# Attention with a gated MLP on one core: turned blocks of p loaded two steps later, the opening reordered, z1 products begun with the last scores, and a scratch of the inverse square root in PSUM

## The chip, the cores and the metric

The kernel runs on one core of one Trainium2 chip. A core has a matrix engine (TensorE, PE in the rows; its weight loads are PEld), VectorE (DVE), ScalarE (ACT), GpSimd (POOL) and SyncE (SP). They run side by side and meet through semaphores; each carries out its own instructions in program order. In this kernel all bulk transfers are issued by SP, which writes a DMA into a queue and goes on, unless the DMA first has to wait for something. The metric is the time on the device in microseconds (us), as the median of several runs; the profile is one execution of its own.

## What is computed

The input x has 2048 rows of 512 floats. Its layer norm goes into two branches, an attention of 32 heads over the last 512 cached keys (W is 512), and a gated MLP that mixes over the rows with a 2048 x 2048 matrix. The result joins them.

```python
def _A_ref(x, k_cache, v_cache, wq, wo):
    q = (x @ wq).reshape(B, Sq, Hq, Dh).transpose(0, 2, 1, 3)
    k, v = k_cache[:, :, Sk - W:], v_cache[:, :, Sk - W:]
    scores = jnp.einsum("bhqd,bhkd->bhqk", q, k) * (Dh ** -0.5)
    p = _softmax(scores, axis=-1)
    o = jnp.einsum("bhqk,bhkd->bhqd", p, v)
    return o.transpose(0, 2, 1, 3).reshape(B, Sq, Hq * Dh) @ wo

def _B_ref(x, w_in, w_sp, b_sp, w_out):
    z = _gelu(jnp.einsum("bsd,df->bsf", x, w_in))
    z1 = z[..., :Fh]
    z2 = _layernorm(z[..., Fh:], axis=-1)
    g = jnp.einsum("ts,bsf->btf", w_sp, z2) + b_sp[None, :, None]
    return jnp.einsum("bsf,fd->bsd", z1 * g, w_out)

xn = _layernorm(x, axis=-1)
s = _A_ref(xn, A_k_cache, A_v_cache, A_wq, A_wo)
g = _silu(_B_ref(xn, B_w_in, B_w_sp, B_b_sp, B_w_out))
return x + s * g
```

## The kernel before

**Products.** All operands are float32. Each is split into a high part (rounded to fp32r by a copy on ACT) and a low part (what is left, a subtraction on POOL or DVE, line 56), and each product is made of three on PE: high by high, high by low, low by high (`mm3`, lines 60 to 62). That is why every product below comes in threes, and why every operand needs one ACT and one POOL or DVE instruction first.

**Layout of the program.** Its five parts follow one another in code order.

1. The opening (lines 296 to 348): x is loaded into `sacc`, 16 tiles of 128 rows. `ln_stats` takes mean and variance on DVE, `rsqrt` lays out a chain of small DVE instructions (two to four elements a partition) for the inverse root, and `tick` lets a few of them go between larger work. `ln_apply` normalizes in place, `ln_flip` transposes on PE and splits into xh (ACT) and xl (DVE). `z1_piece(i, 0)` makes the first of two column halves of tile i's z1; `gelu` is applied to it much later. `split_piece` makes high and low parts of a piece of a weight that `load_piece` had brought into a buffer `raw`.
2. The step loop (lines 350 to 385), t from -7 to 532. A head has 4 blocks of 512 rows, a block 4 steps; there are 512 steps that have a score. A full step holds twelve products of 512 columns: three of `qproj` for the block 7 steps ahead, three of `score`, three of `pv` (12 steps behind) and three of `outp` (17 behind). Pieces of the weights have their own table (lines 289 to 294): piece k of head h is split at step 16 h plus an offset, and its load is issued eight steps earlier.
3. The z stage (lines 444 to 457): 16 tiles, two halves of 344 columns each. `z_product` on PE, `z_gelu` on ACT with the statistics on DVE, and for each pair of tiles `z_norm`: the chain of the inverse root, then two `tensor_scalar` (line 437). `z_split` makes z_h on ACT and z_l on POOL.
4. The mix stage: the 2048 x 2048 matrix by z2 in `mix`, into new PSUM pools that take the place of the old ones, so the first products wait until the z stage's PSUM tiles have been read.
5. The end of each row tile: gate, transposes, `project`, silu, out.

**The way of p.** A score's softmax numerator `prob` (ACT) has to be transposed before it can be a weight of `pv`. `turn(t - 1)` (lines 228 to 243), the last thing in step t, transposes 32 x 32 squares on DVE into a buffer `pB` (four of them) and issues its write to a DRAM block `p_dram`. After the fourth tile of a block it also issues four loads (line 242) that gather the whole block into `pL` (two buffers, 1 MB each). `shares` (ten steps behind a score) splits one quarter of pL into pT_h (ACT) and pT_l (POOL), and `pv` uses it two steps later. The four loads wait for the block's last write to land. SP carries out its instructions in order, so all that stands behind them waits as well: the next writes, the loads of weight pieces, the writes of s and z1.

**The output sum.** `outp` goes into a PSUM tile, and DVE adds it into `sacc`, scaled by the row's softmax sum (line 276). A PSUM tile of `ps_step` (four of them) is free when that has been done, and scores, outp and the z1 products share them.

**z1's second half.** From step `Z1` on, one `z1_piece(t - Z1, 1)` stands in each step (line 373): twelve products of 344 columns, a copy on ACT, a write to DRAM that SP issues (line 197). Before, `Z1` is NSTEP + 2, 514. `turn` still comes after it in the same step, as `pv` and `outp` run on to the end of the loop.

## Time and profile before

| | |
|---|---|
| median of 3 runs | 1937.86 us (1936.36 to 1940.21) |
| the profiled execution | 1932.73 us, its span 1931.0 |
| DVE busy | 1314.0 us, 68%, 2336 instructions |
| ACT busy | 1023.2 us, 53%, 2199 instructions |
| POOL busy | 944.3 us, 49%, 742 instructions |
| SP's DMA queue | 355.33 MB, 70.6% of 16 engines' span |
| granted clock of PE, mean | 0.997 |

The span runs from the first to the last instruction. The matrix engine's share stands with the prediction. Products are pipelined, so a row's duration on PE is longer than the distance from one product to the next; the pace is read from start times. In the timeline a row gives start, duration, engine, line, operation, what it writes and reads, the tile's form, how many equal ones were joined (x4), and in brackets how long the engine had been idle just before and what released it. In the list of waits a row gives the engine and line that waited, what it waited for, the total in us, how many times, and the longest. `SPq` and `PEld` are SP's issue of DMAs and PE's weight loads. The windows give, for a stretch of time, each engine's busy time, then PE's clock, the share in which the DMA engines were busy, and GB/s. The names of tiles in rows are those of the program: `ps` stands for tiles of `ps_step` and, by name, `ps_a` for those of `ps_acc`.

### The profile page before, as it was taken

What the parts mean: (1) busy time and instruction counts of PE and PEld (TensorE: products, weight loads), DVE (VectorE), ACT (ScalarE), POOL (GpSimd) and SP (SyncE); (2) the same over time, 40 slices, a digit from 0 to 9 for tenths busy, and PEclk for the clock granted to TensorE, in tenths of its full rate; (3) what the DMA queues carried; (4) which work ended last, traced back from release to release, by engine and by line L of the source; (5) the groups of instructions that cost most, each with busy time, mean ns of one, the idle gap of its engine ahead of it and who ended that gap; (6) DMA issues with size and microseconds to landing.
All of it is one profiled execution on the core that took longest, in us unless ns stands there. A gap on an engine that the chain in (4) does not pass through costs nothing.

```text
span 1931.0 us, 28085 instructions
## 1 busy us (share of the span) xinstructions
PE 1889.9 (98%) x8914; PEld 1580.9 (82%) x8914; DVE 1314.0 (68%) x2336; ACT 1023.2 (53%) x2199; POOL 944.3 (49%) x742
## 2 busy tenths in 40 slices
PE   6999999999999999999999999999999999999999
PEld 6778878788887788787887777777877898999998
DVE  7678877878877787877787787787887383111112
ACT  3456656556655556656565565555665343324332
POOL 1155555555555555555555555555555155322320
PEclk9999999999999999999999999999999999999999
DMA  4588888888888888888888888878888504333321
GB/s 162 148 213 221 204 214 218 211 209 211 214 212 215 210 214 222 205 210 219 213 207 217 209 207 211 220 201 210 224 206 209 188 28 146 119 102 106 122 70 51
DMA packets 393509, 357.12 MB, mean 185 GB/s; under 512 B 21856, under 2 KB 290400, under 8 KB 393360
## 3 DMA queue, kind: packets, MB, share of 16 engines
q1 hardware_dynamic: 393360, 355.33, 70.6%
q8 instruction: 69, 1.13, 0.3%
q14 instruction: 80, 0.66, 0.1%
HBM read 207.00 MB, written 148.24 MB: 184 GB/s over the span
## 4 chain that ended last, share of the span: by engine, by line
PE 72%; DMA 11%; DVE 8%; ACT 3%; issue 3%; SPq 1%; POOL 0%; DVEq 0%; ACTq 0%; POOLq 0%
DMA p_dram<-pB 10%; PE ps L60 10%; PE ps L61 9%; PE ps L62 9%; PE ps_a L60 9%; PE ps_a L61 9%; PE ps_a L62 9%; PE ps_g L60 4%; PE ps_g L62 4%; PE ps_g L61 4%; DVE pB L234 2%; DVE nm L224 2%; ACT prob L226 2%; DVE sacc L276 2%; PE ps_f L60 1%
## 5 line engine op out<-in xcount | busy, mean ns | idle before, releaser
L56 POOL TENSOR_TENSOR pT_l<-pL,pT_h 128x512 fp32r<-128x512 f32 x507 | 655.4, 1293 | 617.3 <-ACT pT_h L249 553.4
L226 ACT ACTIVATE prob<-ps,nm 128x512 f32<-128x512 f32 x512 | 353.0, 689 | 560.3 <-DVE nm L224 560.3
L234 DVE STREAM_TRANSPOSE pB<-prob 128x512 f32<-128x512 f32 x512 | 359.9, 703 | 102.9 <-DMA p_dram<-pB 102.2
L276 DVE SCALAR_TENSOR_TENSOR sacc<-ps,sums,sacc 128x512 f32<-128x512 f32 x496 | 364.5, 735 | 23.4 <-PE ps L62 22.1
L224 DVE TENSOR_REDUCE nm<-ps 128x1 f32<-128x512 f32 x512 | 334.8, 654 | 1.0 <-PE ps L62 0.8
L249 ACT CAST pT_h<-pL 128x512 fp32r<-128x512 f32 x512 | 316.1, 618 | 21.5 <-DMA pL<-p_dram 15.4
L56 POOL TENSOR_TENSOR wl<-raw,wh 128x512 fp32r<-128x512 f32 (+1 forms) x144 | 180.6, 1256 | 88.3 <-ACT wh L138 88.3
L60 PE MATMUL ps<-wh,qT_h 128*128 128x512 f32 x512 | 211.6, 413 | 10.8 <-DVE sacc L276 8.0
L61 PE MATMUL ps_a<-pT_l,wh 128*128 128x512 f32 x512 | 200.5, 392 | 4.1 <-POOL pT_l L56 4.1
L61 PE MATMUL ps<-wl,qT_h 128*128 128x512 f32 x512 | 201.7, 394 | 0.0
L60 PE MATMUL ps<-wh,oT_h 128*128 128x512 f32 x512 | 199.9, 390 | 1.3 <-ACT z L196 1.1
L60 PE MATMUL ps_a<-xh,wh 128*128 128x512 f32 x512 | 200.4, 391 | 0.0
L60 PE MATMUL ps_a<-pT_h,wh 128*128 128x512 f32 x512 | 199.9, 390 | 0.5 <-ACT pT_h L249 0.5
L61 PE MATMUL ps_a<-xl,wh 128*128 128x512 f32 x512 | 200.1, 391 | 0.0
L62 PE MATMUL ps<-wh,qT_l 128*128 128x512 f32 x512 | 199.7, 390 | 0.0
L62 PE MATMUL ps_a<-xh,wl 128*128 128x512 f32 x512 | 199.6, 390 | 0.0
L61 PE MATMUL ps<-wl,oT_h 128*128 128x512 f32 x512 | 199.6, 390 | 0.0
L62 PE MATMUL ps_a<-pT_h,wl 128*128 128x512 f32 x512 | 199.2, 389 | 0.0
L62 PE MATMUL ps<-wh,oT_l 128*128 128x512 f32 x512 | 198.9, 389 | 0.0
L60 PE MATMUL ps_g<-z_h,xh 128*128 128x344 f32 x512 | 167.4, 327 | 4.4 <-ACT z L425 4.4
L62 PE MATMUL ps_g<-z_h,xl 128*128 128x344 f32 x512 | 164.2, 321 | 0.0
L61 PE MATMUL ps_g<-z_l,xh 128*128 128x344 f32 x512 | 164.0, 320 | 0.0
(107 smaller groups left out, 3059.2 us busy)
## 6 DMA issues: line engine op xcount, KB each, us to landing
p_dram<-pB SPq DMA_DIRECT2D x512, 256.0 KB, 6.1
pL<-p_dram SPq DMA_DIRECT2D x512, 256.0 KB, 5.2
raw<-wh SPq DMA_DIRECT2D x128, 256.0 KB, 6.4
raw<-w_sp SPq DMA_DIRECT2D x56, 256.0 KB, 3.3
z_dram<-z SPq DMA_DIRECT2D x32, 172.0 KB, 1.9
z<-z_dram SPq DMA_DIRECT2D x16, 344.0 KB, 3.2
s_dram<-sacc SPq DMA_DIRECT2D x16, 256.0 KB, 2.0
s_t<-s_dram SPq DMA_DIRECT2D x16, 256.0 KB, 3.5
```

Of the source, the lines that this page charges most:

```text
L56: engine.tensor_tensor(lo, whole, hi.bitcast(F32), op=OP.subtract)
L60: nc.tensor.matmul(ps, lh, rh, start=first, stop=False)
L61: nc.tensor.matmul(ps, lh, rl, start=False, stop=False)
L62: nc.tensor.matmul(ps, ll, rh, start=False, stop=last)
L224: nc.vector.tensor_reduce(nm, ps, axis=AX.X, op=OP.max, negate=True)
L226: nc.scalar.activation(prob[t], ps, AF.Exp, bias=nm, accum_out=sums[b][:, j:j + 1])
L234: nc.vector.transpose(pB.rearrange("p (k q) -> p k q", q=Q), prob.pop(t))
L249: nc.scalar.copy(h, p)
L276: nc.vector.scalar_tensor_tensor(sacc[:, i, :], ps, rs, sacc[:, i, :], op0=OP.mult, op1=OP.add)
```

## The change

It has five parts.

- **Loads of turned blocks.** The four loads of pL leave `turn` and become `turned(b)`. It is called where t is 2 modulo 4, ahead of that step's own `turn`. `turn` of a block's fourth tile stands in the step in which t is 0 modulo 4, so two steps lie between. `shares` and `pv` keep their steps.
- **The inverse root.** `rsqrt` gets its scratch from outside, in two halves, `here` and `there`, and each instruction reads one operand of each. It has thirteen instructions, for one element as for more (eight for one before, eleven for two or more). In the opening both halves are SBUF. In the z stage `there` is a PSUM tile, `tmps`, taken from `ps_acc`. So the z products no longer use `ps_acc`: all of them go through the four tiles of `ps_step`.
- **The opening.** Groups of x tiles are 1, 1, 2, 4, 4, 4 instead of 1, 1 and pairs. The first pieces of w_in and of head 0 have their low parts made on DVE instead of POOL, and the statistics run further ahead (i + 6 for i + 4). The pieces 1 to 3 of head 0 are split inside the step loop, at steps -5, 6 and 9.
- **z1 and the pieces of w_in.** `Z1` is NSTEP - 3, 509, and the write of a z1 piece is issued by ACT. The pieces of w_in for z1's second half and for the z stage are loaded and split at other steps, and share the buffers of other numbers (`FOLLOWS`).
- **Constants.** `halves` and `magic` become one tile `consts`, and a copy of them stands in `tmps`.

```diff
@@ -78,32 +78,32 @@
-    def rsqrt(pool, var, n):
-        v = pool.tile([P, 4], F32, name="rs_v", bufs=6)
-        y = pool.tile([P, 4], F32, name="rs_y", bufs=6)
-        a = pool.tile([P, 4], F32, name="rs_a", bufs=6)
-        v, y, a = v[:, :n], y[:, :n], a[:, :n]
+    def rsqrt(var, y, n, here, there, consts_here, consts_there):
+        (y0, y1, a0), (v, u, a1) = ([m[:, k * n:k * n + n] for k in range(3)] for m in (here, there))
+        stt, mul = nc.vector.scalar_tensor_tensor, nc.vector.tensor_mul
         chain = []
         chains.append(chain)
         def add(f, *args, **kw):
             chain.append(lambda: f(*args, **kw))
-        stt = nc.vector.scalar_tensor_tensor
-        add(stt, v, var, EPS, halves[:, :n], op0=OP.add, op1=OP.mult)
-        add(stt, y.bitcast(I32), v.bitcast(I32), -0.5, magic[:, :n], op0=OP.mult, op1=OP.add)
-        for _ in range(3):
-            if n == 1:
-                add(stt, a, y, v, y, op0=OP.mult, op1=OP.mult)
-            else:
-                add(nc.vector.tensor_mul, a, y, y)
-                add(nc.vector.tensor_mul, a, a, v)
-            add(stt, y, a, 1.5, y, op0=OP.subtract, op1=OP.mult)
-        return y, chain
+        add(stt, v, var, EPS, consts_there[:, :n], op0=OP.add, op1=OP.mult)
+        add(stt, y0.bitcast(I32), v.bitcast(I32), -0.5, consts_here[:, 4:4 + n], op0=OP.mult, op1=OP.add)
+        add(mul, u, v, y0)
+        for old, new in ((y0, y1), (y1, y0), (y0, y)):
+            add(mul, a1, u, old)
+            add(stt, new, a1, 1.5, old, op0=OP.subtract, op1=OP.mult)
+            if new is not y:
+                add(mul, a0, u, old)
+                add(stt, u, a0, 1.5, u, op0=OP.subtract, op1=OP.mult)
+        return chain
+    def set_consts(t):
+        nc.vector.memset(t[:, :4], 0.5)
+        nc.vector.memset(t[:, 4:], float(0x5F3759DF - (1 << 22) - (1 << 31)))
@@ -130,17 +130,21 @@
+    FOLLOWS = {("w", 1): (0, 1, 0, 2), ("w", 2): (1, 3, 2, 3), ("w", 3): (0, 1, 0, 2)}
     def split_piece(key, k, engine):
         n = 512 if key[0] == "h" else NB
-        hi = wp.tile([P, 512], F32R, name=f"wh{k}")
-        lo = wp.tile([P, 512], F32R, name=f"wl{k}")
+        f = FOLLOWS[key][k] if key in FOLLOWS else k
+        hi = wp.tile([P, 512], F32R, name=f"wh{f}")
+        lo = wp.tile([P, 512], F32R, name=f"wl{f}")
         r = raw.pop((key, k))[:, :n]
         nc.scalar.copy(hi[:, :n], r)
         rest(engine, lo[:, :n], r, hi[:, :n])
         wt[key, k] = (hi, lo)
-    GROUPS = [(0, 1), (1, 2)] + [(a, a + 2) for a in range(2, NT, 2)]
+    GROUPS = [(0, 1), (1, 2), (2, 4)] + [(a, a + 4) for a in range(4, NT, 4)]
@@ -149,14 +153,16 @@
     def ln_stats(i):
         a, b = next(g for g in GROUPS if g[0] <= i < g[1])
...
         if i == b - 1:
-            r, chain = rsqrt(stats, mv[a][:, :b - a, 1], b - a)
+            r = stats.tile([P, 4], F32, name="rs_r", bufs=4)
+            here, there = (stats.tile([P, 12], F32, name=f"rs_{k}", bufs=3) for k in range(2))
+            chain = rsqrt(mv[a][:, :b - a, 1], r[:, :b - a], b - a, here, there, consts, consts)
             for j in range(a, b):
                 rx[j] = mv[a][:, j - a, 0:1], r[:, j - a:j - a + 1], chain
@@ -194,7 +200,7 @@
         zmm(ps[:, :NB], i, n, range(2, NC))
         z = zs.tile([P, NB], F32, name="z1")
         nc.scalar.copy(z, ps[:, :NB])
-        nc.sync.dma_start(z1_dram[:, i, n * NB:(n + 1) * NB], z)
+        nc.scalar.dma_start(z1_dram[:, i, n * NB:(n + 1) * NB], z)
@@ -236,11 +242,13 @@
             pD[b] = dram.tile([4, P, 512], F32, name="p_dram", bufs=3)
         nc.sync.dma_start(pD[b][j], pB)
         if j == 3:
-            pL[b] = ap.tile([P, 16, P], F32, name="pL")
-            of = pD.pop(b).rearrange("j (i r) (a f) -> a r (j i) f", i=4, a=4)
-            for a in range(4):
-                nc.sync.dma_start(pL[b][Q * a:Q * a + Q], of[a])
             nc.vector.reciprocal(sums[b], sums[b])
+    def turned(b):
+        pL[b] = ap.tile([P, 16, P], F32, name="pL")
+        of = pD.pop(b).rearrange("j (i r) (a f) -> a r (j i) f", i=4, a=4)
+        for a in range(4):
+            nc.sync.dma_start(pL[b][Q * a:Q * a + Q], of[a])
@@ -278,7 +286,7 @@
             nc.sync.dma_start(s_dram[:, i, :], sacc[:, i, :])
-    T0, T1, Z1 = -QL, NSTEP + OL + 4, NSTEP + 2
+    T0, T1, Z1 = -QL, NSTEP + OL + 4, NSTEP - 3
@@ -289,63 +297,54 @@
     for h in range(1, H):
         for k, d in enumerate((-10, -4, 1, 9)):
             plan(("h", h), k, 16 * h + d)
-    for n, ds in enumerate(((-10, -8, -3, 1), (3, 7, 13, 17), (18, 18, 19, 20))):
+    for k, d in enumerate((-5, 6, 9)):
+        splits.setdefault(d, []).append((("h", 0), 1 + k))
+    for n, ds in enumerate(((-12, -9, -7, -4), (1, 4, 13, 17), (13, 14, 15, 16))):
         for k, d in enumerate(ds):
             plan(("w", 1 + n), k, NSTEP + d)
     load_x(0, 1)
+    load_piece(("w", 0), 0)
     load_x(1, 2)
+    for k in range(1, 4):
+        load_piece(("w", 0), k)
     load_x(2, 4)
-    for k in range(4):
-        load_piece(("w", 0), k)
-    for k in range(2):
+    load_piece(("h", 0), 0)
+    load_x(4, 8)
+    for k in range(1, 4):
         load_piece(("h", 0), k)
-    for a in range(4, NT, 4):
+    for a in range(8, NT, 4):
         load_x(a, a + 4)
...
     ln_stats(0)
-    tick(3)
+    ln_apply(0)
     ln_stats(1)
-    ln_apply(0)
     for k in range(2):
-        split_piece(("w", 0), k, nc.gpsimd)
-    ln_stats(2)
+        split_piece(("w", 0), k, nc.vector)
+    ln_flip(0)
+    for k in range(2, 4):
+        split_piece(("w", 0), k, nc.vector)
     ln_apply(1)
-    ln_flip(0)
-    ln_stats(3)
-    for k in range(2, 4):
-        split_piece(("w", 0), k, nc.gpsimd)
-    split_piece(("h", 0), 0, nc.gpsimd)
-    ln_apply(2)
-    ln_apply(3)
+    for i in (2, 3):
+        ln_stats(i)
     def start(i):
         ln_flip(i + 1)
-        if i == 0:
-            ln_stats(4)
-            ln_stats(5)
-        elif i == 1:
-            tick(11)
-        else:
-            for k in (4, 5):
-                ln_apply(k)
-            for k in (6, 7):
-                ln_stats(k)
+        for j in ((2, 3), (), (4, 5))[i]:
+            ln_apply(j)
+        for j in ((4, 5), (6, 7), (8, 9))[i]:
+            ln_stats(j)
+        tick((0, 11, 0)[i])
     for i in range(3):
         z1_piece(i, 0, lambda: start(i))
-    for k in range(2, 4):
-        load_piece(("h", 0), k)
-    for k in range(1, 4):
-        split_piece(("h", 0), k, nc.gpsimd)
+    split_piece(("h", 0), 0, nc.vector)
@@ -363,8 +362,8 @@
             split_piece(key, k, nc.gpsimd)
         if 0 <= t < NSTEP:
             score(t)
-        if i + 4 < NT:
-            ln_stats(i + 4)
+        if i + 6 < NT:
+            ln_stats(i + 6)
         if i + 2 < NT:
             ln_apply(i + 2)
         if i - 1 < NT:
@@ -381,6 +380,8 @@
             qproj_out(bq, cq)
         if 0 <= bp < NBLK:
             pv_out(bp, cp)
+        if t % 4 == 2 and 0 <= t // 4 - 1 < NBLK:
+            turned(t // 4 - 1)
         if 0 <= t - 1 < NSTEP:
             turn(t - 1)
@@ -410,11 +411,13 @@
     z, zps, zst, zmv = {}, {}, {}, {}
+    tmps = ps_acc.tile([P, 512], F32, name="ps_a")
+    set_consts(tmps[:, :8])
     def z_product(i, n):
-        if n == 2:
-            zps[i, n] = ps_step.tile([P, 512], F32, name="ps_3")
-        else:
-            zps[i, n] = ps_acc.tile([P, 512], F32, name="ps_a")
+        zps[i, n] = ps_step.tile([P, 512], F32, name="ps_3")
         zmm(zps[i, n][:, :NB], i, n, range(NC))
     def z_gelu(i, n):
@@ -431,8 +434,9 @@
             zmv[g] = stats.tile([P, 2, 2], F32, name="mvz")
         nc.vector.bn_aggr(zmv[g][:, j, :], zst[i])
         if j == 1:
-            r, chain = rsqrt(stats, zmv[g][:, :, 1], 2)
-            finish(chain)
+            r = stats.tile([P, 2], F32, name="rz_r")
+            here, o = stats.tile([P, 6], F32, name="rz_h"), 8 + 6 * (g % 2)
+            finish(rsqrt(zmv[g][:, :, 1], r, 2, here, tmps[:, o:o + 6], consts, tmps))
             for k in range(2):
                 nc.vector.tensor_scalar(z[i - 1 + k], z[i - 1 + k], zmv[g][:, k, 0:1], r[:, k:k + 1],
                                         op0=OP.subtract, op1=OP.mult)
```

On SP, in the middle of the attention, the rows from the loads of one block to those of the next but one read so before (L237 is a pB's write into p_dram, L242 the four loads of pL, L131 the load of a weight piece into `raw`; x3 and x4 count equal rows in a row):

```order
L242 DMA pL<-p_dram 32x16x128 x4
L131 DMA raw<-wh 128x512
L237 DMA p_dram<-pB 128x512 x3
L131 DMA raw<-wh 128x512
L237 DMA p_dram<-pB 128x512
L242 DMA pL<-p_dram 32x16x128 x4
L237 DMA p_dram<-pB 128x512 x4
L242 DMA pL<-p_dram 32x16x128 x4
```

and so at the like place of the changed kernel, where L243 is the write and L251 the load:

```order
L251 DMA pL<-p_dram 32x16x128 x4
L243 DMA p_dram<-pB 128x512 x3
L131 DMA raw<-wh 128x512
L243 DMA p_dram<-pB 128x512
L251 DMA pL<-p_dram 32x16x128 x4
L243 DMA p_dram<-pB 128x512 x4
L131 DMA raw<-wh 128x512
L251 DMA pL<-p_dram 32x16x128 x4
```

Before, the loads stand right behind the fourth write of their own block. Now the write just ahead of them is the first of the next block, so that the three before it are the last of theirs.

On PE, at the end of the scores, the rows before read as follows: the last score (`ps_16902`, of qT and the keys in wh_16308), and then `pv` (`ps_a`, of pT) of the same step.

```order
L60 MATMUL ps_16902<-wh_16308,qT_h 128x512
L61 MATMUL ps_16902<-wl_16309,qT_h 128x512
L62 MATMUL ps_16902<-wh_16308,qT_l 128x512
L60 MATMUL ps_a<-pT_h,wh_16478 128x512
L61 MATMUL ps_a<-pT_l,wh_16478 128x512
L62 MATMUL ps_a<-pT_h,wl_16479 128x512
```

In the changed kernel this is the third score from the end (`ps_16826`), followed by the first z1 piece (`ps_16834`, of xh, xl and the w_in piece), of which the first three of twelve products are shown:

```order
L60 MATMUL ps_16826<-wh_16282,qT_h 128x512
L61 MATMUL ps_16826<-wl_16283,qT_h 128x512
L62 MATMUL ps_16826<-wh_16282,qT_l 128x512
L60 MATMUL ps_16834<-wh_16542,xh 128x344
L61 MATMUL ps_16834<-wl_16543,xh 128x344
L62 MATMUL ps_16834<-wh_16542,xl 128x344
```

Twelve products of 344 columns now stand between a score and the `pv` of its step, from the third score before the last on; before, the first of them came three steps after the last score.

On PE, from the z stage to the mix, these are the last products of the z stage and the first of the mix before (z_h and z_l are the halves of z2, xh and xl here those of the mixing matrix; in brackets the engines that a row waits for):

```order
L60 MATMUL ps_a<-wh_17426,xh 128x344
L61 MATMUL ps_a<-wl_17427,xh 128x344
L62 MATMUL ps_a<-wh_17426,xl 128x344
L60 MATMUL ps_g_18205<-z_h,xh 128x344 [waits Activation_49]
L61 MATMUL ps_g_18205<-z_l,xh 128x344 [waits Pool_49]
L62 MATMUL ps_g_18205<-z_h,xl 128x344 [waits Pool_49]
L60 MATMUL ps_g_18206<-z_h,xh 128x344 [waits Activation_49]
```

and now:

```order
L60 MATMUL ps_18118<-wh_17388,xh 128x344
L61 MATMUL ps_18118<-wl_17389,xh 128x344
L62 MATMUL ps_18118<-wh_17388,xl 128x344
L60 MATMUL ps_g_18188<-z_h,xh 128x344 [waits DVE_49]
L61 MATMUL ps_g_18188<-z_l,xh 128x344 [waits Pool_49]
L62 MATMUL ps_g_18188<-z_h,xl 128x344 [waits Pool_49]
L60 MATMUL ps_g_18189<-z_h,xh 128x344
```

The z products now write tiles of `ps_step`, and the mix's first product, whose PSUM bank is the one that held `tmps`, waits for DVE where it waited for ACT.

More of the change, by code (lines that the diff above doesn't have):

```diff
@@ L151, in ln_stats @@
         if i == a:
-            mv[a] = stats.tile([P, 4, 2], F32, name="mv", bufs=6)
+            mv[a] = stats.tile([P, 4, 2], F32, name="mv", bufs=4)
         stt = stats.tile([P, 6], F32, name="stt", bufs=4)
@@ L306, in mixer_kernel @@
     make_identity(nc, ident)
-    halves = const.tile([P, 4], F32, name="halves")
-    nc.vector.memset(halves, 0.5)
-    magic = const.tile([P, 4], F32, name="magic")
-    nc.vector.memset(magic, float(0x5F3759DF - (1 << 22) - (1 << 31)))
+    consts = const.tile([P, 8], F32, name="consts")
+    set_consts(consts)
     bsp = const.tile([P, NT], F32, name="bsp")
```

## The prediction

> **What bounds the kernel now.** I read the page's busy shares first, then the matrix engine's own start times, then the waits.
>
> ```profile
> PE 1889.9 (98%) x8914; PEld 1580.9 (82%) x8914; DVE 1314.0 (68%) x2336; ACT 1023.2 (53%) x2199; POOL 944.3 (49%) x742
> ...
> 702.99 0.39 PE L60 MATMUL ps<-wh,qT_h 128*128 128x512 f32 x1
> 705.72 0.39 PE L60 MATMUL ps<-wh,qT_h 128*128 128x512 f32 x1
> ...
> 125.00 0.50 PE L60 MATMUL ps<-wh,qT_h 128*128 128x512 f32 x1
> 1457.79 0.39 PE L60 MATMUL ps<-wh,qT_h 128*128 128x512 f32 x1
> ```
>
> PE is never idle for long, but 98% says only that products overlap. The score products tell more: there is one per step, all 512 are in the trace, and a step holds twelve 512-column products. An undisturbed step lasts 2.73 us (the second and third row), 0.2275 a product. The last two rows are the scores of steps 27 and 504: 1332.8 us for 477 steps, 2.794 each. At 2.727 they would take 1300.8. So **32.0 us** are lost in the steady part, a few tenths at a time, and the waits say to whom.
>
> ```profile
> DVE pB L234 <- DMA p_dram<-pB: 102.2, 102, 3.7
> PEld ps L60 <- DVE sacc L276: 45.1, 99, 1.6
> SPq L242 <- DMA p_dram<-pB: 508.2, 254, 5.3
> ```
>
> SP stands for 508 us at the pL loads, until the block's last p_dram write has landed. DVE's transposes wait for a pB buffer whose write has not landed. The next score's weights wait for sacc on DVE, which runs late and holds a PSUM buffer. One block shows the chain:
>
> ```profile
> 682.33 0.32 SPq L237 DMA_DIRECT2D p_dram<-pB  x1
> 686.05 1.92 SPq L242 DMA_DIRECT2D pL<-p_dram  x4
> 688.01 0.49 SPq L131 DMA_DIRECT2D raw<-wh  x1
> 688.54 1.44 SPq L237 DMA_DIRECT2D p_dram<-pB  x3
> ...
> 694.03 0.61 ACT L249 CAST pT_h<-pL 128x512 fp32r<-128x512 f32 x1
> ...
> 694.98 0.71 DVE L234 STREAM_TRANSPOSE pB<-prob 128x512 f32<-128x512 f32 x1 [1.07 <-DMA p_dram<-pB]
> ```
>
> The fourth write of a block goes out at 682.33. SP then waits until 686.05, issues four loads, and only at 688.54 issues the next block's first write, which was due one step after 682.33, at 685.1. That write now queues behind 1 MB of loads, and DVE waits for it at 694.98. Counted over all score rows and all 102 waits: 23 of the 118 blocks of four steps have no such wait and lose 1.4 us together; 95 have one and lose 30.0.
>
> **The change, part by part.** *Loads two steps later.* In SP's order one write of the next block now stands between a block's fourth write and its loads, so it goes out on time. The loads follow as soon as the fourth write has landed. That took 3.7 us here behind a bunch of writes; the on-time write comes at 2.73, so the loads start about 3 to 3.7 us after the fourth write, not later than before. What queues behind the loads now is the second write; its buffer is needed again four steps (10.9 us) after it was issued, and the loads take less:
>
> ```profile
> DMA to landing us min/median/max: 3.2/5.2/7.7
> ...
> 590.00:591.00 1.00, 1.00 (x6) 0.81 (x6) 0.33 (x1) 1.00 (x4) 0.00 (x0) 1.00 1.15 201
> 596.00:597.00 1.00, 1.00 (x6) 0.84 (x5) 1.00 (x3) 0.95 (x3) 0.00 (x0) 1.00 0.02 6
> ```
>
> The first row is pL's landing; with 1.9 us for four issues, all has come some 7 us after the first. The windows show that the DMA engines are full during the loads and empty (share 0.02) for a moment in each block, so they are not the bound. DVE's wait should go. What is late next is pL itself: here it was needed 11.7 us after the fourth write (694.03), and should now come at about 11. Bounds: nothing, if the wait only moves, to 32. I take **28**, near the blocks without a wait, which lose 0.06 each.
>
> *z1 products with the last scores.*
>
> ```profile
> 1475.96 0.39 PE L60 MATMUL ps<-wh,qT_h 128*128 128x512 f32 x1
> 1482.97 0.32 PE L60 MATMUL ps<-wh,xh 128*128 128x344 f32 x1
> 1499.68 0.45 ACT L196 COPY z<-ps 128x344 f32<-128x344 f32 x1 [9.23 <-DMA z_dram<-z]
> 1500.18 0.50 PE L60 MATMUL ps<-wh,oT_h 128*128 128x512 f32 x1 [1.09 <-ACT z L196]
> 1532.58 0.32 PE L60 MATMUL ps<-wh,xh 128*128 128x344 f32 x1
> ...
> 1533.73 0.93 POOL L56 TENSOR_TENSOR wl<-raw,wh 128x344 fp32r<-128x344 f32 x1 [1.35 <-ACT wh L138]
> ```
>
> From step 504 (1457.79) to the first product of the z stage (1532.58) pass 74.8 us. The work is 162 products of 512 columns (36.9) and 192 of 344 columns at 0.158 (30.3), 67.2 together: 7.6 lost. The last score starts at 1475.96, the first z1 product only at 1482.97; between, PE follows DVE. Later ACT waits 9.23 us for a z_dram write that sat in SP's queue behind pL's wait, and PE 1.09 with it. Now the z1 products start five steps earlier, beside the last three scores, and their writes are issued by ACT, past SP's queue; that puts 32 issues on ACT, which is half idle. Steps 505 to 508 stay short of PE work, some 1.5 us. Gain **6** (3 to 7.6). Against it: z1 now ends at step 524, with only 3.4 us of out products and 1.6 of z products before the last piece of w2 is needed. That piece stands sixth among low parts on POOL at 0.93 each, so PE waits about 2 us. Before, such waits cost 1.4 in the whole z stage (32 products of 12 times 0.158 from 1532.58 would end at 1593.2; the last ends at 1594.6, two products ahead of the 1594.88 below): **-0.5** (-2 to 0).
>
> *The rsqrt chain over PSUM.*
>
> ```profile
> 1572.28 1.19 DVE L437 TENSOR_SCALAR z<-z,mvz,rs_y 128x688 f32<-128x688 f32 x2
> 1581.35 1.18 DVE L437 TENSOR_SCALAR z<-z,mvz,rs_y 128x688 f32<-128x688 f32 x2
> ...
> 1585.81 1.66 POOL L56 TENSOR_TENSOR z_l<-z,z_h 128x688 fp32r<-128x688 f32 x1
> ...
> 1585.90 1.59 DVE L94 SCALAR_TENSOR_TENSOR rs_y<-rs_v,magic 128x2 int32<-128x2 int32 x1
> ...
> 1594.88 0.32 PE L62 MATMUL ps_g<-z_h,xl 128*128 128x344 f32 x1
> 1599.61 0.65 PE L60 MATMUL ps_g<-z_h,xh 128*128 128x344 f32 x1 [4.41 <-ACT z L425]
> ```
>
> DVE takes 9.07 us for two tiles, PE 48 products of 0.158, 7.6. A chain instruction on two elements lasts 1.59 us, as long as POOL's 1.66 that it started beside. PE pays at the end only: 4.41 us until ACT's late gelu frees a PSUM bank. With one operand in PSUM the chain should run unhindered, 13 instructions in place of 11. The Trainium skill (SBUF — State Buffer, Who interferes with whom) says that a VectorE instruction with at most one SBUF input stays clear of GpSimd, but that tensor_scalar from SBUF to SBUF may not: by it the chain goes free and L437 can still be held up.
> But the chain's scratch is PSUM, and the first mix product now waits for the chain's last instruction. Its price comes from an undisturbed tile:
>
> ```profile
> 1541.39 0.32 PE L62 MATMUL ps_a<-wh,xl 128*128 128x344 f32 x1
> 1541.75 0.46 ACT L425 ACTIVATE z<-ps_a 128x344 f32<-128x344 f32 x1 [1.44 <-PE ps_a L62]
> 1542.24 0.52 DVE L426 BATCH_NORM_STATS2 stz<-z 128x6 f32<-128x344 f32 x1 [1.37 <-ACT z L425]
> 1542.79 0.21 DVE L432 BATCH_NORM_AGGREGATE mvz<-stz 128x2 f32<-128x12 f32 x1
> 1543.04 0.16 DVE L94 SCALAR_TENSOR_TENSOR rs_v<-mvz,halves 128x2 f32<-128x2 f32 x1
> 1543.23 0.16 DVE L94 SCALAR_TENSOR_TENSOR rs_y<-rs_v,magic 128x2 int32<-128x2 int32 x1
> ```
>
> 1.65 us from the last product to the chain, 13 times 0.195 (about the spacing of the last two rows), 0.2 to release PE: 4.4. Before, it was 1594.88 to 1599.61, 4.7. One wait takes the other's place: **+0.3** (-1 to +1). The chip has no row of small DVE operations on PSUM; between 0.16 and twice that, the chain costs up to 2 us more. The z products have four PSUM buffers, not eight: three products of 1.9 us of slack for ACT, enough while DVE keeps pace.
>
> *The opening.*
>
> ```profile
> 3.51 0.69 DVE L154 BATCH_NORM_STATS2 stt<-sacc 128x6 f32<-128x512 f32 x1 [2.61 <-DMA sacc<-x]
> 33.61 0.55 DVE L166 TENSOR_SCALAR sacc<-sacc,mv,rs_y 128x512 f32<-128x512 f32 x1
> 34.07 0.69 DVE L56 TENSOR_TENSOR xl<-ps,xh 128x512 fp32r<-128x512 f32 x1
> ...
> 34.30 0.90 PE L177 MATMUL ps<-ident,sacc 128*128 128x128 f32 x4 [0.21 <-DVE sacc L166]
> 71.73 0.40 PE L60 MATMUL ps<-wh,qT_h 128*128 128x512 f32 x1
> ```
>
> Low parts leave POOL for DVE, and DVE sets the pace. Up to tiles 4 and 5 it now has from 3.5: eight statistics (0.9 with the aggregate), four chains (2.4), six scalings (0.55), four xl (0.69), four w low parts (about 0.5), 24.9 together, to 28.4. PE then turns tile 4 at 28.0 and, at 2.95 a tile, tile 6 at 34.3. Before it was 34.30. I take **0** (-2 to +2); each 3.4 us at half clock costs 1.5 of that.
>
> *First blocks.* Steps 6 to 26 (71.73 to 125.00) took 53.3 for 201 products, 45.7. Most of the 7.5 lost is the latency of the first turned blocks, which stays: **1.5** (0 to 5).
>
> The sum is 28 + 6 - 0.5 + 0.3 + 0 + 1.5 = 35.3, from the profiled 1932.73 (span 1931.0): 1897.4. The runs' median stands 5.1 above that execution. If that is more of the same waits, it goes too; I add half, and predict **1900**.
>
> **Rivals.** *pL becomes the wait* (0.12): pL at 11 stands close to the 11.7 at which it is needed; if ACT's wait brings back half of the loss, 1914. *The wait only moves to the second write* (0.05): the steady 28 stay lost, 1928, and three fifths of that chance lie within 0.2%. *The z stage stays at DVE's pace* (0.07): if the chain or L437 is still held up, 1.5 us a pair over eight pairs, less the 5.7 of slack of the buffers, and a late end: 8 more, 1908. The page's rule on tensor_scalar speaks for this one. *Slower* (0.04): pT of a block is used nine steps, 24.5 us, after its last score. About 5 to the transpose, 0.7, 11 until pL is there and 2 to split it make 18.7. From 5.8 us later on, each further us would be paid once in nine steps, 57 times in all (512 over nine); 0.62 beyond that point uses up the 35.3, and 1.7 beyond it gives 1897 + 97, 1994.
>
> **How the numbers follow.** The forecast has 0.72; its own range is 1891 to 1910. With the second and third rivals and the unknown costs, 8 in 10 lie in 1889 to 1918. Faster by over 0.2% (3.9 us, about what a measurement here can tell): 0.93; within: 0.03; slower: 0.04.
>
> **What would show it.** Right: scores 2.73 apart nearly everywhere from step 27 to 504; DVE's wait for p_dram under 20 us; the first z1 product before the last score; chain instructions of 0.2 us; the first mix product waiting over 4 us, now for DVE. Wrong: steps still at 2.8, or long waits of ACT or POOL for pL; L437 some 9 us apart; PE waiting inside the z stage.

## The result, and the profile after

| | before | after |
|---|---|---|
| median of 4 runs each | 1938.10 us (1936.36 to 1940.21) | 1890.73 us (1890.06 to 1892.77) |
| the profiled execution's span | 1931.0 us | 1888.9 us |

The ratio is 0.9757, with a 95% interval of 0.974 to 0.9774. The changed kernel is 47.4 us faster. The forecast was 1900; the time lies 0.3 us under its own range (1891 to 1910) and inside the wider one (1889 to 1918).

The page of the changed kernel gives the busy shares, and the trace the scores of steps 27 and 504, which bound the steady part:

```profile
PE 1860.3 (98%) x8914; PEld 1589.6 (84%) x8914; DVE 1308.9 (69%) x2344; ACT 1024.9 (54%) x2199; POOL 938.7 (50%) x737
...
121.98 0.39 PE L60 MATMUL ps<-wh,qT_h 128*128 128x512 f32 x1
1422.59 0.39 PE L60 MATMUL ps<-wh,qT_h 128*128 128x512 f32 x1
```

PE's share reads 98% as before, and still 42 us are gone. The two scores stand 1300.6 us apart, where they stood 1332.8 apart. All 119 blocks of four steps between them take 10.91 us.

In the list of waits (line, what it waited for, total in us, times, longest) DVE's pB now waits for p_dram twice, 0.9 us in all, where it had waited 102 times. These rows stand out now; the last is from SP's own list:

```profile
DVE sacc L284 <- PE ps L62: 194.7, 365, 2.5
ACT pT_h L257 <- DMA pL<-p_dram: 12.8, 20, 2.0
SPq L251 <- DMA p_dram<-pB: 128.9, 108, 3.3
```

DVE now waits for PE, 194.7 us in this row where it was 22.1, and has time to spare. SP still stands at the loads, but for 129 us in place of 508. One block in the timeline of SP and ACT:

```profile
686.42 0.32 SPq L243 DMA_DIRECT2D p_dram<-pB  x1
686.78 0.43 SPq L131 DMA_DIRECT2D raw<-wh  x1
688.33 0.32 SPq L243 DMA_DIRECT2D p_dram<-pB  x1
688.92 2.54 SPq L251 DMA_DIRECT2D pL<-p_dram  x4
...
698.71 0.61 ACT L257 CAST pT_h<-pL 128x512 fp32r<-128x512 f32 x1
```

The fourth write goes out at 686.42. The next block's first write follows at 688.33, on time, and only then the loads. pT_h follows at 698.71, 12.3 us after the fourth write, with no wait behind it in brackets. Over all blocks pL has landed 11.9 us after the fourth write (median).

At the end of the z stage, PE and DVE:

```profile
1494.94 0.43 PE L61 MATMUL ps<-wl,xh 128*128 128x344 f32 x1 [1.85 <-POOL wl L56]
...
1550.36 0.64 DVE L441 TENSOR_SCALAR z<-z,mvz,rz_r 128x688 f32<-128x688 f32 x1
1553.90 0.32 PE L62 MATMUL ps<-wh,xl 128*128 128x344 f32 x1
1557.66 0.16 DVE L91 SCALAR_TENSOR_TENSOR rz_r<-ps_a,rz_h 128x2 f32<-128x2 f32 x1
1557.88 0.42 PE L60 MATMUL ps_g<-z_h,xh 128*128 128x344 f32 x1 [3.66 <-DVE rz_r L91]
1557.93 0.64 DVE L441 TENSOR_SCALAR z<-z,mvz,rz_r 128x688 f32<-128x688 f32 x1
```

DVE's pairs stand 7.57 us apart (1550.36 to 1557.93), PE's pace, where they took 9.07. The first mix product now waits for the chain's last instruction, 3.66 us.

Where the 42.1 us of the span came from, by stages read from PE's starts (in us; the runs named e are described below):

| stage | before | after | e1: loads alone | e3: all but the loads |
|---|---|---|---|---|
| start to score 6 | 71.7 | 71.0 | 70.5 | 69.5 |
| scores 6 to 27 | 53.3 | 51.0 | 50.8 | 52.6 |
| scores 27 to 504 | 1332.8 | 1300.6 | 1300.6 | 1346.8 |
| score 504 to the first z product | 74.8 | 68.8 | 67.9 | 71.9 |
| first to last z product | 61.8 | 62.5 | 61.8 | 64.0 |
| last z product to the last product | 331.8 | 330.7 | 330.8 | 330.8 |
| to the end | 4.7 | 4.3 | 4.7 | 4.3 |

The stage from the last z product on is shorter by 1.1, but e1, which leaves the inverse root as it was, has 1.0 of it. What differs is the clock behind the wait of the first mix products. These are ten us around the end of that wait, of the kernel before, of e1 and of the changed kernel (each engine's busy time, then PE's clock, the DMA share, GB/s):

```profile
1598.00:1608.00 10.00, 8.39 (x38) 8.39 (x39) 8.43 (x22) 4.75 (x8) 4.95 (x3) 0.66 0.01 3
1555.00:1565.00 10.00, 8.08 (x42) 8.08 (x43) 8.08 (x22) 4.44 (x8) 4.74 (x3) 0.83 0.02 6
1556.00:1566.00 10.00, 8.12 (x42) 8.13 (x43) 4.51 (x14) 4.01 (x7) 5.88 (x5) 0.83 0.38 111
```

A mean clock of 0.66 is 6.8 of the ten us at half clock, and one of 0.83 is 3.4.

### The profile page after: what moved, and what is told of

Its sections match the earlier page's. It is cut to its first block, busy times and chain, and to the rows that moved or that the text cites. A ratio compares the mean times of both kernels' runs of the same rounds, so it can differ in the third digit from the quotient of the medians.

```text
span 1888.9 us, 28086 instructions
## 1 busy us (share of the span) xinstructions
PE 1860.3 (98%) x8914; PEld 1589.6 (84%) x8914; DVE 1308.9 (69%) x2344; ACT 1024.9 (54%) x2199; POOL 938.7 (50%) x737
## 4 chain that ended last, share of the span: by engine, by line
PE 95%; DVE 2%; issue 1%; POOL 1%; ACT 1%; DMA 1%; SPq 0%; ACTq 0%; POOLq 0%; DVEq 0%
PE ps L61 14%; PE ps L60 14%; PE ps L62 14%; PE ps_a L61 12%; PE ps_a L60 12%; PE ps_a L62 12%; PE ps_g L60 5%; PE ps_g L62 4%; PE ps_g L61 4%; PE ps_f L60 1%; PE ps_f L62 1%; PE ps_f L61 1%; PE ps_u L535 1%; PE ps L183 0%; POOL wl L56 0%
## 5 line engine op out<-in xcount | busy, mean ns | idle before, releaser
L284 DVE SCALAR_TENSOR_TENSOR sacc<-ps,sums,sacc 128x512 f32<-128x512 f32 x496 | 370.6, 748 | 194.7 <-PE ps L62 194.7
L56 POOL TENSOR_TENSOR wl<-raw,wh 128x512 fp32r<-128x512 f32 (+1 forms) x139 | 176.0, 1268 | 88.4 <-ACT wh L142 73.9
L60 PE MATMUL ps<-wh,qT_h 128*128 128x512 f32 x512 | 201.4, 393 | 1.0 <-DVE sacc L282 1.0
```

Of the source, the lines that this page charges most:

```text
L56: engine.tensor_tensor(lo, whole, hi.bitcast(F32), op=OP.subtract)
L60: nc.tensor.matmul(ps, lh, rh, start=first, stop=False)
L284: nc.vector.scalar_tensor_tensor(sacc[:, i, :], ps, rs, sacc[:, i, :], op0=OP.mult, op1=OP.add)
```

## The experiments

Each is compared with the kernel before, run on the same chip (medians 1935.8 to 1938.4).

**e1: the loads alone.** In the kernel before, the loads leave `turn`:

```diff
     def turn(t):
...
         if j == 3:
-            pL[b] = ap.tile([P, 16, P], F32, name="pL")
-            of = pD.pop(b).rearrange("j (i r) (a f) -> a r (j i) f", i=4, a=4)
-            for a in range(4):
-                nc.sync.dma_start(pL[b][Q * a:Q * a + Q], of[a])
             nc.vector.reciprocal(sums[b], sums[b])
+
+    def turned(b):
+        pL[b] = ap.tile([P, 16, P], F32, name="pL")
+        of = pD.pop(b).rearrange("j (i r) (a f) -> a r (j i) f", i=4, a=4)
+        for a in range(4):
+            nc.sync.dma_start(pL[b][Q * a:Q * a + Q], of[a])
...
+        if t % 4 == 2 and 0 <= t // 4 - 1 < NBLK:
+            turned(t // 4 - 1)
         if 0 <= t - 1 < NSTEP:
             turn(t - 1)
```

> The kernel before with one edit: the four loads of pL are issued two steps later; all else as before. Theory A (order on SP: the steady loss is the next block's first write standing behind the loads, and nothing else of the change is needed): scores 27 to 504 take 1301 us (1300 to 1303), DVE's wait of pB for p_dram falls from 102 us to under 5, the first blocks (scores 6 to 27) gain 1 to 3, the end of attention and the z stage stay as before; 1895 to 1903 in all. Theory B (the steady gain also needs the other parts of the change): scores 27 to 504 stay over 1310, the time over 1910.

Measured: 1890.07 us, ratio 0.9746 (0.973 to 0.9763), five us under the range of theory A. The trace has these two scores, 27 and 504:

```profile
121.35 0.39 PE L60 MATMUL ps<-wh,qT_h 128*128 128x512 f32 x1
1421.97 0.39 PE L60 MATMUL ps<-wh,qT_h 128*128 128x512 f32 x1
```

1300.6 us: theory A, and B falls. This one edit gives as much as the whole change (1890.73). DVE's wait of pB for p_dram is 4.1 us in three waits. The expectation that the end of attention stays as before failed: from score 504 to the z stage it shrank by 6.9, from 74.8 to 67.9.

**e3: everything but the loads.** In the changed kernel:

```diff
-        if t % 4 == 2 and 0 <= t // 4 - 1 < NBLK:
-            turned(t // 4 - 1)
         if 0 <= t - 1 < NSTEP:
             turn(t - 1)
+        if t % 4 == 0 and 0 <= t // 4 - 1 < NBLK:
+            turned(t // 4 - 1)
```

> The changed kernel with the loads of pL put back right behind the block's fourth write; all else as changed. Theory A: the steady loss comes back, scores 27 to 504 take 1330 to 1336 us, the first blocks lose 1 to 3, the end of attention keeps its gain as z1's writes go through ACT's queue: 1922 to 1932 in all. Theory B: scores 27 to 504 stay under 1315, the time under 1910.

Measured: 1942.98 us, ratio 1.002 (1.0008 to 1.0033). DVE's wait is back:

```profile
DVE pB L240 <- DMA p_dram<-pB: 116.0, 110, 3.3
PEld ps L60 <- DVE sacc L284: 60.6, 124, 1.5
```

The steady part loses 46.0 us, which is 14 more than in the profiled execution before; the order on SP is the same. Why it is more was not settled. That this loss varies shows in the runs before, which spread from 1933.6 to 1943.7, while the changed kernel's spread 2.7. The end of attention keeps a part of its gain, 2.9 us up to the z stage (74.8 to 71.9). The z stage then takes 2.2 more than before: PE waits 1.86 for POOL's wl, as in the changed kernel, and runs at half clock for 3.4 us behind that wait, which costs another 1.5.

**e2: a buffer more in place of later loads.** In the kernel before:

```diff
-        pB = ap.tile([P, 512], F32, name="pB", bufs=4)
+        pB = ap.tile([P, 512], F32, name="pB", bufs=5)
-    zs = att.enter_context(tc.tile_pool(name="zs", bufs=2))
+    zs = att.enter_context(tc.tile_pool(name="zs", bufs=1))
```

> The kernel before with the loads where they were, but five pB buffers instead of four; to make room, the copies of z1 pieces have one buffer instead of two. Of the 102 waits of DVE for a pB buffer only one was longer than a step (3.66 us), so a buffer more hides all but 0.9 us of 102. Theory A (DVE's wait for pB is the whole link from the late write to PE): scores 27 to 504 take 1301 to 1304 us, 1897 to 1910 in all, with some loss at z1. Theory C (the burst of loads on the DMA engines or SP's blocked queue costs by other ways too): scores 27 to 504 take 1315 or more, 1918 or more in all.

Measured: 1934.82 us, ratio 0.9978 (0.9967 to 0.999). Between 125 and 1457 us, the list of waits and, in the 400 us from 400 to 800, the row of the windows (PE's busy time and records first) of this kernel, and below them the same row of e1:

```profile
DVE pB L234 <- DMA p_dram<-pB: 15.3, 29, 1.1
PEld ps L60 <- DVE sacc L274: 0.6, 1, 0.6
PE ps L60 <- DVE sacc L274: 0.2, 1, 0.2
...
400.00:800.00 400.00, 400.00 (x1724) 323.79 (x1723) 325.36 (x541) 239.76 (x540) 229.52 (x181) 1.00 0.87 213
400.00:800.00 400.00, 400.00 (x1762) 330.52 (x1761) 331.60 (x551) 244.53 (x552) 236.14 (x184) 1.00 0.91 218
```

PE has no wait left worth a microsecond, as theory A wanted, and is busy for all of the 400 us at the full clock. Yet it gets through 1724 products in place of 1762. The products themselves start 232.2 ns apart in place of 227.2, and 477 steps of 12 products by 5 ns are the 28.6 us that remain. The time lies where theory C put it, but the waits that C would need are not there. Neither theory had products that follow each other more slowly without a wait.

**e6 and e7: is it the place of the tiles?** e6 is e1 with the two lines of e2's diff. e7 is the kernel before with

```diff
-        pB = ap.tile([P, 512], F32, name="pB", bufs=4)
+        pB = ap.tile([P, 512], F32, name="pB", bufs=6)
-    rawp = raws.enter_context(tc.tile_pool(name="rawp", bufs=6))
+    rawp = raws.enter_context(tc.tile_pool(name="rawp", bufs=5))
-    zs = att.enter_context(tc.tile_pool(name="zs", bufs=2))
+    zs = att.enter_context(tc.tile_pool(name="zs", bufs=1))
```

> The kernel before with the loads two steps later, and besides the five pB buffers and the one z1 copy buffer of the run e2_before_pb5. There PE had no wait left between scores 27 and 504, but its products stood 232.2 ns apart on average in place of 227.2, all 119 blocks alike. Theory F (the place of the tiles in SBUF, which five buffers shift, slows the products): the products stand 232 ns apart here too, scores 27 to 504 take 1327 to 1331 us, 1915 to 1925 in all. Theory G (the timing of the loads and of the engines against PE does it): 227 ns, 1300 to 1303 us, 1888 to 1896 in all.

> The kernel before with the loads where they were and six pB buffers; to make room, five raw buffers in place of six and one copy buffer for z1. DVE's wait for pB should be gone altogether. Theory F (place in SBUF): the products' spacing depends on the layout, so that with this one it may be 227 again, and then scores 27 to 504 take 1301 to 1304 us. Theory G (timing): 231 to 233 ns and 1325 to 1332 us as with five buffers, since the loads stand where they stood. Theory A alone (DVE's wait was all): 1301 to 1304 us.

Measured: e6 1921.25 us, ratio 0.9926 (0.9911 to 0.9941); e7 1936.33, ratio 1.0004 (0.9994 to 1.0014). The windows from 400 to 800, e6 and then e7:

```profile
400.00:800.00 400.00, 400.00 (x1724) 323.84 (x1723) 324.31 (x539) 239.35 (x540) 229.61 (x180) 1.00 0.92 213
400.00:800.00 400.00, 400.00 (x1724) 323.81 (x1723) 324.64 (x539) 238.93 (x539) 229.24 (x180) 1.00 0.88 213
```

1724 again in both, with the loads on time in e6 and late in e7. Each of the three runs loses 28.4 to 28.9 us in the steady part, 0.24 in every block. The order of the loads makes no difference to the spacing, so theory G falls by e6, though e7 alone has the number that G gave. In e7 the tiles from `sacc` to pB lie 2048 bytes a partition (one raw buffer) lower than in e2 and e6, pL and the tiles behind it where they lie there, and each kind of product has the same spacing to within 1 ns.

**e8 and e9: 32 bytes.** Both put a pad ahead of `sacc`, e8 in e2, e9 in the changed kernel:

```diff
+    nc.gpsimd.memset(sp.tile([P, 8], F32, name="pad"), 0.0)
     sacc = sp.tile([P, NT, D], F32, name="sacc")
```

> The run e2_before_pb5 (loads where they were, five pB buffers, one z1 copy buffer) with a pad of 32 bytes a partition ahead of sacc. In e2, e6 and e7, all with products at 232 ns, the tiles behind sacc (qT, pT, oT) begin 32 bytes off a multiple of 64 while x and the weight pieces begin on one; in before, after and e1, with 227 ns, all of them have the same remainder. The pad makes it the same again. Theory F2 (PE is slowed when its two operands differ in that remainder): 227 ns, and with DVE's wait hidden by the fifth buffer scores 27 to 504 take 1301 to 1305 us if that wait is the whole link from the late write to PE (theory A): 1896 to 1908 in all. If the late loads cost by other ways too (ACT waited 88 us for pL in e2): 227 ns in most steps, but 1308 us or more. Without F2: 232 ns and 1329 us again.

> The changed kernel with the same pad of 32 bytes, which here makes the remainders differ (sacc, qT, pT and oT on a multiple of 64, x and the weight pieces 32 off). Theory F2: products at 232 ns, scores 27 to 504 take 1327 to 1331 us, 1919 to 1925 in all. Without it: 227 ns, 1889 to 1893.

Measured: e9 1914.74 us, ratio 0.9893 (0.9879 to 0.9908), which is 24 us over the changed kernel; one of its four executions took 1919.3, the others 1914.1 to 1914.8. e8 1935.71, ratio 0.9984 (0.9968 to 1.0); one of its ten took 1922.8, the others 1934.4 to 1936.4, and why is open. The windows, e8 and then e9:

```profile
400.00:800.00 400.00, 400.00 (x1712) 321.46 (x1711) 321.74 (x535) 236.47 (x535) 228.73 (x178) 1.00 0.76 210
400.00:800.00 400.00, 400.00 (x1728) 324.21 (x1727) 325.26 (x540) 239.65 (x541) 231.03 (x180) 1.00 0.89 213
```

e9 settles that place alone does it: 32 bytes between `wh` and x on one side and the attention's tiles on the other, and the products start 231.7 ns apart. In it, those of `qproj`, on two tiles that the pad doesn't move against each other, keep 226.7, while those with qT, pT or oT take 231 to 236. But e8 refutes the rule that led there: all remainders by 64 agree in it, and its products take 233.9 ns, the slowest of all. What rule of addresses decides is open. The traces do show that PE's two reads for a product are not the whole of it. In e8 the products of `qproj` take 234.7 ns on average, though x and the weights lie at the addresses that they have in the kernel before, where the median is 227. So something beside these reads slows PE there, most likely another engine or a DMA at one of the tiles that moved; which, was not tested.

As a test of DVE's wait, e8 agrees with e2: no wait of PE is left in it, and all 38.0 us that it loses are the spacing.

**e4 and e5: where the edge is.** In the changed kernel, e4 puts the loads behind two writes of the next block, and e5, with the second pair of lines, behind three:

```diff
-        if t % 4 == 2 and 0 <= t // 4 - 1 < NBLK:
+        if t % 4 == 3 and 0 <= t // 4 - 1 < NBLK:
             turned(t // 4 - 1)
```
```diff
-        if t % 4 == 2 and 0 <= t // 4 - 1 < NBLK:
-            turned(t // 4 - 1)
+        if t % 4 == 0 and 0 <= t // 4 - 2 < NBLK:
+            turned(t // 4 - 2)
```

> The changed kernel with the loads another step later, so that two writes of the next block stand ahead of them. pL then lands some 2.7 us later, 14.6 after the fourth write in place of 11.9. Theory D (the slack of 5.5 us before PE is hit, as worked out for the slower rival): ACT waits some 2 us a block for pL, 200 to 300 us in all, PE does not lose: 1888 to 1895. Theory E (ACT works in order, so a late pT_h delays the exponentials behind it, and PE loses with it): 0.5 us or more a block, 1950 or more.

> The changed kernel with the loads two steps later still, behind three writes of the next block. In e4, one write later, the loads went out 1.3 us later and PE lost nothing. Here they go out some 7.5 us after the fourth write and all of pL has landed 15.3 after it, where the slower rival of the prediction put the edge at 16.8. Theory D: ACT waits some 2 to 3 us a block for pL, 250 to 400 us in all, PE does not lose: 1888 to 1897. Theory E (ACT's order hands the wait on to the exponentials): 0.3 us or more a block, over 1925.

Measured: e4 1890.10 us, ratio 0.9748 (0.9732 to 0.9764); e5 2198.23, ratio 1.1356 (1.1339 to 1.1373). ACT's wait, in e4 and then in e5, and a stretch of e5 on SP and ACT:

```profile
ACT pT_h L257 <- DMA pL<-p_dram: 45.2, 45, 3.6
ACT pT_h L257 <- DMA pL<-p_dram: 488.2, 115, 7.1
...
700.66 12.77 SPq L243 DMA_DIRECT2D p_dram<-pB  x4
713.53 2.03 SPq L251 DMA_DIRECT2D pL<-p_dram  x4
...
721.39 0.62 ACT L257 CAST pT_h<-pL 128x512 fp32r<-128x512 f32 x1 [3.52 <-DMA pL<-p_dram]
721.92 0.68 ACT L232 ACTIVATE prob<-ps,nm 128x512 f32<-128x512 f32 x1
```

In e4 pL has landed 12.6 us after the fourth write (median; 11.9 in the changed kernel, 14.6 expected) and PE loses nothing in the steady part: theory D, though ACT's wait is far below the 200 us that it named. In e5 the loads went out 10.0 us after the fourth write, not 7.5, as the third of the writes ahead of them goes out only at 9.3 (medians; 7.6 in the changed kernel). pL has landed 16.9 us after at the least and 19.3 in the median, and the steady part loses 290 us, 2.4 a block. ACT stands at pT_h, the exponentials behind it come late, and so do the next writes: theory E. The edge lies between 12.6 and 16.9; as the latter was measured in a kernel that already runs late, it is not placed more closely.

**b1, b2 and b4: the end of the z stage.** b1 takes one more tile ahead of tmps, so that tmps lies in the fourth bank and not in the first:

```diff
+    nc.vector.memset(ps_acc.tile([P, 512], F32, name="ps_a")[:, :4], 0.0)
     tmps = ps_acc.tile([P, 512], F32, name="ps_a")
```

> The changed kernel with one line more: a tile of ps_acc is taken and set before tmps, so that tmps lies in bank 3 and the first mix product's bank was last used long before. Theory H (the first mix product waits for nothing but the chain's last read of its bank): its 3.66 us go, and so does the half clock that follows (3.5 us of it, 1.75 lost), 5.4 us: 1884 to 1887. Theory I (the wait only moves to the low parts of the last z tiles, or the half clock comes anyhow): 1889 to 1892.

Measured: 1885.73 us, ratio 0.974 (0.9726 to 0.9755). Its last z products and first mix product on PE, and the window from 1550 to 1580 of the changed kernel and then of b1 (behind the engines' busy times: PE's clock, the DMA share, GB/s):

```profile
1551.73 0.32 PE L62 MATMUL ps<-wh,xl 128*128 128x344 f32 x1
1551.89 0.32 PE L60 MATMUL ps_g<-z_h,xh 128*128 128x344 f32 x1
...
1550.00:1580.00 30.00, 26.34 (x160) 26.03 (x159) 9.75 (x29) 9.80 (x16) 12.95 (x9) 0.94 0.49 153
1550.00:1580.00 30.00, 30.00 (x195) 29.98 (x194) 8.78 (x25) 11.63 (x20) 18.60 (x14) 1.00 0.58 178
```

Theory H: the mix follows at once, and the clock stays at 1.00 where the wait had brought 0.94. The Trainium skill (TensorE: Matmul & The Clock Gate, What's actually happening) says that PE falls to half its clock after an idle window of about 3.4 us; with a wait of 3.66 us here, and none in b1, the trace agrees. But a shorter wait can do it as well. In the z stage PE waits for POOL's wl for 1.85 us in the changed kernel and for 1.87 in e4, at the same place; only in e4 is there a stretch at half clock behind it. The wait in e4, and the window behind it in the changed kernel and then in e4:

```profile
1494.95 0.54 PE L61 MATMUL ps<-wl,xh 128*128 128x344 f32 x1 [1.87 <-POOL wl L56]
...
1495.00:1499.00 4.00, 4.00 (x26) 4.00 (x27) 1.25 (x3) 2.20 (x3) 0.00 (x0) 1.00 0.62 196
1495.00:1499.00 4.00, 4.00 (x16) 4.00 (x17) 0.52 (x1) 1.74 (x3) 0.00 (x0) 0.57 0.63 195
```

e4's z stage takes 1.5 us more for it (64.0 to 62.5), and e3's has the same. So times that differ by one or two us can differ by such a stretch alone.

b2 leaves tmps in SBUF:

```diff
-    tmps = ps_acc.tile([P, 512], F32, name="ps_a")
+    tmps = stats.tile([P, 20], F32, name="tmps", bufs=1)
```

> The changed kernel with tmps in SBUF, so that both operands of the chain are SBUF, as before the change; four PSUM buffers for the z products as changed; the mix's banks are free, as in b1_free_bank (1885.7). If DVE's pace of 9.07 us a pair then holds PE up, as the third rival of the prediction has it: 8 us more than b1_free_bank, 1891 to 1897. If the chain over PSUM is worth nothing: 1884 to 1888.

Measured: 1887.24 us, ratio 0.9746 (0.9731 to 0.976), 1.5 over b1 and inside the range that was given for a chain that is worth nothing. In the trace its z stage takes 2.4 us more than b1's. Chain instructions on two elements last long again, and PE waits twice for a PSUM buffer that ACT has yet to read:

```profile
1542.37 0.88 DVE L91 SCALAR_TENSOR_TENSOR tmps<-mvz,tmps 128x2 f32<-128x2 f32 x1
1543.28 1.59 DVE L91 SCALAR_TENSOR_TENSOR rz_h<-tmps,consts 128x2 int32<-128x2 int32 x1
...
1541.17 0.43 PE L60 MATMUL ps<-wh,xh 128*128 128x344 f32 x1 [0.98 <-ACT z L428]
1549.84 0.42 PE L60 MATMUL ps<-wh,xh 128*128 128x344 f32 x1 [0.83 <-ACT z L428]
```

DVE's pairs stand 9.2 us apart again. So the scratch in PSUM does free the chain, but with four PSUM buffers it is worth some 2 us and not 8: they hide most of DVE's lag. The eight that the kernel before had for the z products hid it better still: there, and in e1, the z stage took 61.8 with the slow chain, against 62.5 in the changed kernel.

b4 is b1 with four of the w_in pieces' low parts on DVE:

```diff
-            split_piece(key, k, nc.gpsimd)
+            split_piece(key, k, nc.vector if key == ("w", 2) and k > 1 or key == ("w", 3) and k % 2 else nc.gpsimd)
```

> b1_free_bank, and besides four of the eight low parts of w_in pieces for the z stage (pieces 2 and 3 of the first half, 1 and 3 of the second) are made on DVE, which has some 1.2 us idle there, in place of POOL. If PE's wait of 1.85 us at the second product of the z stage is POOL's row of six low parts, it goes, with 0.2 to 0.4 us of what follows: 1.5 to 2.5 us under b1_free_bank. If PE then waits for ACT's high parts or for DVE instead: 0 to 0.5 under it.

Measured: 1882.55 us, ratio 0.9727 (0.9713 to 0.9742), the fastest of all, and faster than both kernels. Its z stage is 0.8 us shorter than b1's, since PE's wait of 1.85 for POOL becomes one of 1.0 for DVE. The medians differ by 3.2, more than either forecast and more than the traces account for. b1's four executions rank by their granted clock, 1883.4 at 1.000 (the profiled one), 1885.2 at 0.999 and 1886.3 at 0.998 twice, so stretches at half clock, as e4 shows them behind the wait of 1.87, may be the rest; that was not tested.

## Why the prediction was right, and where not

*The steady part* was forecast at 28 of the 32.0 lost, and 32.2 came. The mechanism was the one told: the first write behind the loads, and DVE waiting for it. e1 and e3 show that the order on SP decides. e2 and e8 point to DVE's wait as the way to PE: with a fifth buffer PE has no wait, though the writes are late. They do not prove it, as PE is slower there, which gives the other engines 0.24 us more in each block of e2 and 0.32 in e8. The size was 4 too small because a rest of 4 was kept, and none is left. pL landed at 11.9 after the fourth write and was no new wait; the first rival had put the edge there, but PE's two steps of reserve, and e4, put it later.

*The last scores and z1* were forecast at 6, and from score 504 to the z stage 6.0 came (74.8 to 68.8). **But the step had the wrong cause, and that the number fits is luck.** "Now the z1 products start five steps earlier" is not what brings it: e1, with z1 where it was, brings 6.9, more than the whole change. e3, with z1 moved and the loads right behind the fourth write, brings 2.9. So the move is worth something only where the loads stand as before; beside the later loads it costs 0.9 here (68.8 in the changed kernel, 67.9 in e1) and 0.7 in the z stage. The cause that the runs leave is the loads. Of e1's 6.9, 2.2 come ahead of score 511, where the steady part's waits went on, and 4.7 behind it. In that second stretch PE waited three times before: 0.23 for DVE's sacc, 0.85 for POOL's pT_l and 1.09 for ACT's copy of z1, the last of them told in the prediction with ACT's 9.23 us for a z_dram write "that sat in SP's queue behind pL's wait". e1 has none of the three, and ACT's longest wait for such a write is 5.5 there. How much of the 4.7 each is worth was not tested. The wait for POOL's sixth low part, foreseen at about 2, came as 1.85, and the z stage lost 0.7 where 0.5 was put.

*The inverse root* did what was said within the chain: instructions of 0.15 to 0.17 us, DVE at PE's pace, and a wait of 3.66 for DVE in place of 4.41 for ACT (4.4 forecast; the sign of being right had said over 4). `tensor_scalar` took 0.64 us in the median before and after (at most 0.88), so it was not what held DVE up. The stage behind gained 1.1 where 0.3 was put, but this is the half clock of 3.4 in place of 6.8 us, which e1 has without the new chain: no gain of the chain is shown there. The rival "The z stage stays at DVE's pace" did not come about; b2 brings it about and gives it 2.4 in place of 8, so its size was wrong.

*The opening* was put at 0, and 0.8 came. In its working, tile 4 at 28.0 and two tiles of 2.95 make 33.9 and not 34.3; PE turned tile 4 at 26.2 and tile 6 at 33.9. The spread from run to run is as large as the gain: the six kernels here with the old opening reach score 6 after 70.5 to 72.0 us, 71.0 on average, the eight with the new one after 69.2 to 71.0, 69.8 on average. So it is worth some 1.2.

*First blocks:* 2.2 came for 1.5, and e1 has 2.5 from the loads alone.

*From execution to median,* half of 5.1 us was added. The changed kernel's profiled execution took 1891.0, its median 1890.7. So none of the gap is left, as it would be if it was made of the same waits; with one profiled execution of each kernel this is not shown.

By the executions' own times 41.7 came (1932.7 to 1891.0) where 35.3 was forecast; with the half gap of 2.6 and 0.3 from that execution to the median, this is the 9.3 between 1900 and 1890.7. But the five parts are not worth what their terms say: the late loads alone give it all, and the other four come to nothing (1890.73 to 1890.07): some 1.2 in the opening against z1's 1.6, a chain whose lag the eight buffers had hidden, and a wait that only changed its owner.

*The slower rival* needs more delay than the change has. It put the edge at 16.8 after the fourth write (5.8 us behind 11); e5, at 16.9 or later, is over it, e4, at 12.6, is not. The changed kernel stands two writes away from an order that costs 300 us.

## What to carry to other kernels

In a queue that works in order, a transfer that waits belongs behind the urgent ones that are due meanwhile; find the place by moving it until what it feeds becomes the wait, and stay a step short of that. Test each part of a change alone: here one of five gave everything, and a stage's gain came from another part than the one that had been written into it. And when a buffer count changes, compare the spacing of products in stretches without waits, since an experiment can be slowed by where its tiles come to lie.

## What was not expected of the hardware

The place of tiles in SBUF sets the pace of PE's products, though PE is never idle and its clock is full. Four different sets of distances between x, the weights and the attention's tiles gave 231.7 to 233.9 ns for a 512-column product, the original distances 227.2 in the six kernels that kept them and had no waits. 32 bytes cost 24 us of 1890. The Trainium skill (SBUF — State Buffer, SBUF: two separate sides) says that PE never waits on anyone. e8 speaks against that: its `qproj` products are slowed from 227 to 234.7 ns while their own operands lie where they lay. Whether it is another engine or a DMA that PE meets was not shown.
